# Attention beside a gated MLP on one core: gate weights on another queue, the first block split, and a new order of the attention stage

## The chip, the cores and the metric

The kernel runs on one core of one Trainium2 chip. The time is the device time of one execution in microseconds (us); the figure for a kernel is the median over its runs. The engines are named as the profile names them: PE is TensorE (PEld its weight loads), DVE is VectorE, ACT is ScalarE, POOL is GpSimd and SP is SyncE, which here only issues DMA transfers.

## What is computed

Both branches take the same normalised input `xn` (2048 tokens, 512 features, bf16); their outputs and the input itself are added.

```python
xn = layernorm(x)                                    # no weights
# branch A: 32 heads of 16, each query sees itself and the 255 keys before it
q, k, v = split(xn @ wqkv)
p = softmax(where(0 <= i - j < 256, q @ k.T * 16 ** -0.5, -1e9))
A = (p @ v) @ wo
# branch B: F = 1376, Fh = 688
z = gelu_tanh(xn @ w_in)
z1, z2 = z[:, :688], layernorm(z[:, 688:])
g = w_sp @ z2 + b_sp[:, None]                        # w_sp is 2048 x 2048
B = (z1 * g) @ w_out
out = x + A + B
```

## The kernel before

Tokens are cut into 16 blocks of 128. The program has two stages, and in both every engine's instructions run in the order in which they are written; nothing is rescheduled.

**The z stage** (the first 53 us). For each block `n` the input is loaded (`load_block` and `load_x`, SP's queue), its mean and variance are taken (`stats`, L257: two DVE instructions, then `rpow`, L117: one DVE instruction for variance plus epsilon and one POOL power for the reciprocal root), it is normalised (`norm`, L263, DVE, which waits for POOL), transposed to `xnT` (`transpose_x`, L274, four PE transposes into a PSUM tile and one ACT copy; from block 6 on a DMA transpose instead) and multiplied with the two halves of `w_in` (`do_z`, L284: four chunks of 128 features, each as two matmuls of 512 and 176 columns, then one ACT activation). Half 1 of z is normalised again (`z2_stats`, `z2_norm`, DVE and POOL). `w_in` comes in four transfers (`load_win`, L206): half 1 in chunks 0-1 and 2-3, which the first z needs, and half 0 in two more. One-element memsets into `w_in_sb` (L318) and `wqkv` (L332) hold later transfers back until DVE has come to them. The first nine projections of q, k and v run between the later blocks.

Ahead of it stands a warm-up: ten matmuls of 512 columns on a tile of zeros that DVE has set, then block 0's transposes, then three more.

The head of the z stage, as it is written:

```python
warm_up(N_WARM[0]); stats(0); ...
stats(1); norm(0); transpose_x(0); warm_up(N_WARM[1])
norm(1); transpose_x(1); do_z(0, 1)
stats(2); norm(2); stats(3); ...
do_z(1, 1); transpose_x(2); stats(4); norm(3); do_z(0, 0)
```

**The attention stage** (from 53 us on) runs the list of words in `ORDER` one by one. Only PE's work is ordered by it directly; the other engines take their parts in the same order.

- a number: so many steps of the mix `w_sp @ z2` (`mix`, L394; 512 steps of 344 columns, a DVE operation behind every sixteenth)
- `qTTe`: a group of scores, tile TT (four 128x128 blocks), one half of the heads (`scores`, L476): eight or more matmuls on 32 rows each, four at a time, into two PSUM tiles, and two exponentials on ACT. The pool of these tiles has three buffers
- `mTT`: the tile's masks, on POOL for diagonal blocks and on DVE for the far ones
- `a`, `A`, `B`, `C`: one group of values (`values`, L529), column-split matmuls, then on DVE and POOL the division (`divide`); the letter names the PSUM it goes to: `a` the one-buffer bank `ps_y`, the others a tile of the scores' pool
- `t`: the transpose of a finished value group (DVE)
- `p`, `P`: one projection, into `ps_y` or (`P`) a tile of the scores' pool
- `o`, `O`: half of an output block (four matmuls with `wo`, or six with `w_out`, a DVE addition and the store), in `ps_y` or in the scores' pool

Of the kernel before, what the change touches and what calls it, by code (L numbers as in the profile page):

```python
# [8 lines left out]
P = 128  # L9
BF = mybir.dt.bfloat16  # L10
F32 = mybir.dt.float32
# [8 lines left out]
FH = 688  # L20
FQ = FH // 2
NB = S_TOK // P
NDC = D // P
# [8 lines left out]
X_DMA = 6  # L32
LAST = 128
ONB = 4
N_WARM = (10, 3)

# [8 lines left out]


ORDER = """
pv11 Pk03 q000 1 pq03 2 q001 2 pq10 1 q010 9 m00 q011 1 pk10 q020 3 m01 2 a00 1 q021 10 q030  # L50
pk11 4 m02 q031 10 q040 2 pv03 q041 4 m03 t 1 pk12 q050 6 m04 1 q051 1 a01 3 q060 pk13 3 m05
q061 4 a02 1 q070 8 q071 a03 1 t 3 q080 pv10 2 m07 2 q081 pq11 3 m06 1 q090 pq12 4 q091 a04 3
m08 q100 2 pk20 2 q101 9 q110 pv12 1 t 1 m10 3 q111 1 pv13 1 m09 q120 5 pq21 q121 3 t 1 a05 m11
q130 2 m12 8 q131 pq20 4 q140 t t 2 pk21 q141 3 A06 a07 A10 q150 4 m13 7 q151 2 pq13 q160 m14 6
a11 q161 3 t 6 q170 1 t pv20 1 t q171 3 m16 5 m15 3 q180 4 pq23 q181 1 m17 8 q190 t a12 6 q191 1
pk23 3 m18 3 q200 6 m19 4 q201 a13 C14 B15 q210 t 2 pv21 4 q211 5 m20 3 q220 2 pk22 Pv23 3 m21
q221 3 pq31 q230 10 q231 pq30 2 m23 q240 4 pq22 2 m22 q241 7 t 1 q250 a16 1 t 3 q251 1 m24 2 t 3
Pv30 6 q260 pk32 3 t q261 2 A20 a17 A21 q270 11 q271 m26 pk30 4 q280 t 10 q281 2 pv31 4 q290 1
m25 2 m28 7 q291 2 pv22 q300 1 m27 9 q301 m29 6 A22 m30 a23 q310 8 q311 3 t 5 pk33 q320 1 m31
Pq33 3 a24 q321 2 t 7 t q330 3 pq32 t Pk31 q331 pv33 4 q340 2 m32 3 m33 3 q341 4 pv32 m34 1 q350  # L60
2 t 10 q351 3 a30 A25 t A26 a27 q360 10 q361 3 t o 1 q370 1 m35 1 o m36 q371 3 m37 5 t q380 3 o
1 q381 4 o q390 A31 a32 1 t 2 t 1 t q391 8 m39 q400 3 o 1 q401 o 1 O q410 2 O 1 o 3 m38 q411 1 o
q420 1 m40 5 A33 a34 q421 O t 2 O 1 q430 2 t m42 m41 o 1 q431 2 o q440 m43 4 O 2 O 1 A35 a36
q441 3 O m44 O o o t 5 A37 1 t O O t 2 o o 1 O O 6 O 1 O O O O O
"""


# [1 line left out]
def kernel(  # L69
# [12 lines left out]
    nc = tc.nc  # L82
# [6 lines left out]
    xnT = pers.tile([P, NDC, S_TOK], BF, name="xnT")  # L89
# [18 lines left out]
    ps_s = ctx.enter_context(tc.tile_pool(name="ps_s", bufs=3, space=bass.MemoryType.PSUM))  # L108
    ps_y = ctx.enter_context(tc.tile_pool(name="ps_y", bufs=1, space=bass.MemoryType.PSUM))
    ps_g = ctx.enter_context(tc.tile_pool(name="ps_g", bufs=1, space=bass.MemoryType.PSUM))  # L110
    sml = ctx.enter_context(tc.tile_pool(name="sml", bufs=3))
# [5 lines left out]
    def rpow(dst, var, n):  # L117
        v = sml.tile([P, NB], F32, name="rs_v")
        nc.vector.tensor_scalar(out=v[:, :n], in0=var, scalar1=LN_EPS, scalar2=None, op0=ALU.add)  # L119
        nc.gpsimd.tensor_tensor(out=dst, in0=v[:, :n], in1=negh[:, :n], op=ALU.pow)  # L120
# [57 lines left out]
    with tc.tile_pool(name="win_pool", bufs=1) as winp, tc.tile_pool(  # L178
        name="xsp", bufs=8
    ) as xsp, tc.tile_pool(name="xnp", bufs=4) as xnp:  # L180
        w_in_sb = winp.tile([P, NDC, F], BF, name="w_in_sb")
        zeros = winp.tile([P, 512], BF, name="zeros")
        nc.vector.memset(zeros[:], 0.0)  # L183
        nc.vector.memset(fmask[:], 1.0)
        nc.vector.memset(esel[:], 1.0)
        make_identity(nc, ident[:])
        xs_tiles = {}
# [3 lines left out]
        def load_block(n):  # L191
            if n % 2 == 0:
                xs_pairs[n // 2] = xsp.tile([P, 2, D], BF, name="xs")
            xs_tiles[n] = xs_pairs[n // 2][:, n % 2, :]
            nc.sync.dma_start(out=xs_tiles[n], in_=x2[n * P : (n + 1) * P, :])
# [7 lines left out]
            for j in range(2):  # L203
                xs_tiles[2 * n2 + j] = xs[:, j, :]

        def load_win(half, c0, c1):  # L206
            nc.sync.dma_start(
                out=w_in_sb[:, c0:c1, half * FH : (half + 1) * FH],
                in_=B_w_in[c0 * P : c1 * P, half * FH : (half + 1) * FH].rearrange(
                    "(c p) f -> p c f", p=P  # L210
                ),
            )

        load_block(0)
        load_block(1)
        load_win(1, 0, 2)
        load_block(2)
        load_win(1, 2, 4)
        load_block(3)
        warm = sml.tile([P, 1], F32, name="warm")  # L220
# [3 lines left out]
            out=fmask[:], in_=fmask[:], pattern=[[-1, P]], compare_op=ALU.is_gt,  # L224
# [3 lines left out]
            out=esel[:], in_=esel[:], pattern=[[-32, 4]], compare_op=ALU.is_ge,  # L228
# [3 lines left out]
            out=esel[:], in_=esel[:], pattern=[[32, 4]], compare_op=ALU.is_ge,  # L232
# [15 lines left out]
        def warm_up(n):  # L248
            wt = ps_s.tile([P, 2, 512], F32, name="warm_t", tag="S")
            for i in range(n):  # L250
                nc.tensor.matmul(  # L251
                    wt[:, 0, :], lhsT=zeros[:, 0:P], rhs=zeros[:], start=True, stop=True
                )

        xn_tiles = {}

        def stats(n):  # L257
            st = sml.tile([P, nc.vector.BN_STATS_DIM], F32, name="st")
            nc.vector.bn_stats(out=st[:], in_=xs_tiles[n])
            nc.vector.bn_aggr(out=mvx[:, n, :], in_=st[:])  # L260
            rpow(rstdx[:, n : n + 1], mvx[:, n, 1:2], 1)

        def norm(n):  # L263
            xn = xnp.tile([P, D], BF, name="xn")
            nc.vector.tensor_scalar(
                out=xn[:], in0=xs_tiles[n], scalar1=mvx[:, n, 0:1],
                scalar2=rstdx[:, n : n + 1], op0=ALU.subtract, op1=ALU.mult,
            )
            if n >= X_DMA:
                nc.sync.dma_start_transpose(out=xnT[:, :, n * P : (n + 1) * P], in_=xn[:])  # L270
            else:
                xn_tiles[n] = xn

        def transpose_x(n):  # L274
            xn = xn_tiles.pop(n)
            pool, tag = (ps_y, "y") if n == 1 else (ps_g, "g")
            tp = pool.tile([P, NDC, P], BF, name="tp", tag=tag)
            for c in range(NDC):
                nc.tensor.transpose(  # L279
                    out=tp[:, c, :], in_=xn[:, c * P : (c + 1) * P], identity=ident[:]  # L280
                )
            nc.scalar.copy(out=xnT[:, :, n * P : (n + 1) * P], in_=tp[:])

        def do_z(n, half):  # L284
            zp2 = ps_s.tile([P, 2, 512], F32, name="zs", tag="S")
            zp = zp2[:].rearrange("p a q -> p (a q)")
            f0 = half * FH
            for c in range(NDC):
                for lo, hi in Z_RANGES:
                    nc.tensor.matmul(  # L290
                        zp[:, lo:hi],
                        lhsT=xnT[:, c, n * P : (n + 1) * P],
                        rhs=w_in_sb[:, c, f0 + lo : f0 + hi],
                        start=(c == 0),
                        stop=(c == NDC - 1),
                    )
            dst = z1_all if half == 0 else z2_all
            nc.scalar.activation(out=dst[:, n, 0:FH], in_=zp[:, 0:FH], func=ACT.Gelu_apprx_tanh)  # L298

# [14 lines left out]
        early = [(kind, 0, grp) for grp in range(3) for kind in "kqv"]  # L314

        warm_up(N_WARM[0])
        stats(0)
        nc.vector.memset(w_in_sb[0:1, 0, 0:1], 0.0)  # L318
        load_x(2)
        load_win(0, 0, 2)  # L320
        load_win(0, 2, 4)
        stats(1)
        norm(0)
        transpose_x(0)
        warm_up(N_WARM[1])
        norm(1)
        transpose_x(1)
        do_z(0, 1)
        stats(2)
        norm(2)  # L330
        stats(3)
# [3 lines left out]
        for n2 in range(4, NB // 2):  # L335
            load_x(n2)
        do_z(1, 1)
        transpose_x(2)
        stats(4)
        norm(3)  # L340
        do_z(0, 0)
        nc.vector.tensor_reduce(
            out=emask[:, 0:1], in_=esel[:], op=ALU.add, axis=mybir.AxisListType.X
        )
        nc.vector.tensor_scalar(
            out=emask[:, 1:2], in0=emask[:, 0:1], scalar1=-1.0, scalar2=1.0,
# [232 lines left out]
    def finish():  # L579
# [9 lines left out]
        out=w_out_sb[:, 0:5, :], in_=B_w_out[0:640, :].rearrange("(c p) n -> p c n", p=P)  # L589
# [52 lines left out]
```

## Time and profile before

| | us |
|---|---|
| median of 3 runs | 265.3 (265.15 to 265.53) |
| the profiled execution | 265.24 |
| its span (first to last instruction) | 263.5 |
| PE busy in the span | 256.9 |
| ACT busy | 205.5 |
| DVE busy | 197.9 |
| POOL busy | 122.0 |
| first z matmul | 6.91 |
| first score group | 55.0 |

"Busy" for PE counts a matmul from its start to its modelled end, so it says that the engine had work in hand, not that it ran at its peak. The chain that ended last is followed back from the last instruction to whatever released it; an engine with nearly all of that chain sets the time. In the timeline a row gives start, duration, engine, line and operation, what is written from what is read, and in brackets the idle time in front of it with its releaser.

### The profile page before, as it was taken

What the parts mean: (1) busy time and instruction counts of PE and PEld (TensorE: products, weight loads), DVE (VectorE), ACT (ScalarE), POOL (GpSimd) and SP (SyncE); (2) the same over time, 40 slices, a digit from 0 to 9 for tenths busy, and PEclk for the clock granted to TensorE, in tenths of its full rate; (3) what the DMA queues carried; (4) which work ended last, traced back from release to release, by engine and by line L of the source; (5) the groups of instructions that cost most, each with busy time, mean ns of one, the idle gap of its engine ahead of it and who ended that gap; (6) DMA issues with size and microseconds to landing.
All of it is one profiled execution on the core that took longest, in us unless ns stands there. A gap on an engine that the chain in (4) does not pass through costs nothing.

```text
span 263.5 us, 7433 instructions
## 1 busy us (share of the span) xinstructions
PE 256.9 (98%) x3166; PEld 143.4 (54%) x3199; DVE 197.9 (75%) x384; ACT 205.5 (78%) x233; POOL 122.0 (46%) x140
## 2 busy tenths in 40 slices
PE   8999999999999999999999999999999999999995
PEld 3665665654546465555565456655564454545542
DVE  5899999667786888788797778897869563786542
ACT  2777767699999999999988989988898996782000
POOL 4334446116542573768553556455468453355100
PEclk9999999999999999999999999999999999999999
DMA  7892233940505073130360322661329263636432
GB/s 215 277 301 42 42 56 68 166 161 2 109 4 112 7 105 41 43 82 13 69 82 2 80 44 41 76 51 38 82 86 179 59 132 94 140 93 151 107 85 77
DMA packets 61233, 23.83 MB, mean 90 GB/s; under 512 B 52321, under 2 KB 60689, under 8 KB 61201
## 3 DMA queue, kind: packets, MB, share of 16 engines
q1 hardware_dynamic: 60720, 23.06, 41.1%
q8 instruction: 25, 0.41, 0.7%
q10 hardware_dynamic: 432, 0.30, 0.4%
q0 software_dynamic: 48, 0.00, 0.3%
q14 instruction: 8, 0.06, 0.1%
HBM read 8.41 MB, written 2.10 MB: 40 GB/s over the span
## 4 chain that ended last, share of the span: by engine, by line
PE 97%; issue 1%; DVE 1%; DVEq 0%
PE gf L402 31%; PE zs L290 14%; PE S L496 12%; PE m L151 10%; PE o_t L549 8%; PE fo L439 8%; PE m L135 6%; PE fo L433 5%; PE warm_t L251 2%; PE tp L279 1%; DVE xnT L444 0%; DVE o_c L565 0%; DVE zeros L183 0%; DVEq L565 0%
## 5 line engine op out<-in xcount | busy, mean ns | idle before, releaser
L504 ACT ACTIVATE E<-S 128x1024 bf16<-128x1024 f32 x180 | 168.9, 1042 | 16.9 <-PE S L496 9.1
L402 PE MATMUL gf<-z_all,wspT 128*128 128x344 bf16 x512 | 95.1, 311 | 0.1
L515 POOL TENSOR_SCALAR_AFFINE_SELECT E<-E 128x1024 bf16<-128x1024 bf16 x64 | 79.3, 1262 | 31.3 <-ACT E L504 31.1
L402 PEld LDWEIGHTS <-wspT 128*128 128x128 bf16 x512 | 44.1, 98 | 35.9 <-issue 15.4
L520 DVE TENSOR_TENSOR E<-E,fmask 128x1024 bf16<-128x1024 bf16 x56 | 53.0, 973 | 2.4 <-ACT E L504 2.3
L571 POOL TENSOR_TENSOR o_norm<-o_c,rsum 128x256 bf16<-128x256 f32 x32 | 21.5, 672 | 61.9 <-DVE rsum L569 59.2
L290 PE MATMUL zs<-w_in_sb,xnT 128*128 128x512 bf16 (+1 forms) x249 | 39.1, 307 | 0.4
L496 PE MATMUL S<-q_ring,k 32*128 32x128 bf16 (+2 forms) x760 | 37.2, 267 | 0.0
L298 ACT ACTIVATE z_all<-zs 128x688 bf16<-128x688 f32 x32 | 23.8, 744 | 12.5 <-PE zs L290 12.5
L151 PE MATMUL m<-xnT,wqkv 128*128 128x512 bf16 x111 | 31.5, 380 | 1.0 <-issue 0.2
L290 PEld LDWEIGHTS <-xnT 128*128 128x128 bf16 x256 | 22.2, 98 | 14.9
L409 DVE SCALAR_TENSOR_TENSOR z_all<-gf,b_all,z_all 128x344 bf16<-128x344 f32 x32 | 18.1, 567 | 14.6 <-PE gf L402 14.6
L565 DVE STREAM_TRANSPOSE o_c<-o_t 128x512 f32<-128x512 f32 x32 | 22.3, 698 | 7.2 <-PE o_t L549 6.5
L496 PEld LDWEIGHTS <-k 32*128 32x128 bf16 x760 | 12.7, 92 | 25.9 <-issue 25.2
L444 DVE TENSOR_TENSOR xnT<-fo,xnT 128x512 bf16<-128x512 f32 (+2 forms) x17 | 11.2, 659 | 17.0 <-PE fo L439 15.3
L549 PE MATMUL o_t<-E,v 128*32 128x128 bf16 (+1 forms) x1080 | 23.4, 238 | 0.0
L439 PE MATMUL fo<-w_out_sb,uT 128*128 128x512 bf16 (+2 forms) x101 | 23.3, 366 | 0.1
L549 PEld LDWEIGHTS <-v 128*32 128x32 bf16 x1080 | 19.2, 97 | 5.1 <-issue 4.6
L171 DVE TENSOR_TENSOR k<-m,emask 128x1024 bf16<-128x1024 f32 x13 | 15.8, 1218 | 3.1 <-PE m L151 3.0
L120 POOL TENSOR_TENSOR rstdx<-rs_v,negh 128x1 f32<-128x1 f32 x16 | 10.2, 640 | 17.0 <-DVE rs_v L119 14.5
L151 PEld LDWEIGHTS <-wqkv 128*128 128x128 bf16 x128 | 11.7, 98 | 11.6 <-issue 1.7
L135 PE MATMUL m<-wqkv,xnT 128*128 128x128 bf16 x256 | 16.9, 219 | 0.2 <-DVE o_c L565 0.2
(51 smaller groups left out, 174.6 us busy)
## 6 DMA issues: line engine op xcount, KB each, us to landing
xnT<-in_A_x_dram SPq DMA_DIRECT2D x4, 512.0 KB, 4.6
out_dram<-xnT SPq DMA_DIRECT2D x13, 128.0 KB, 1.8
xs<-in_A_x_dram SPq DMA_DIRECT2D x6, 256.0 KB, 6.8
wqkv<-in_A_wqkv_dram SPq DMA_DIRECT2D x1, 1536.0 KB, 6.4
w_in_sb<-in_B_w_in_dram SPq DMA_DIRECT2D x4, 344.0 KB, 4.2
w_out_sb<-in_B_w_out_dram SPq DMA_DIRECT2D x1, 640.0 KB, 6.1
xs<-in_A_x_dram SPq DMA_DIRECT2D x4, 128.0 KB, 2.7
wo_sb<-in_A_wo_dram SPq DMA_DIRECT2D x1, 512.0 KB, 4.9
```

What stands on the lines that cost most here:

```text
L135: nc.tensor.matmul(m[:, j * P : (j + 1) * P], lhsT=xnT[:, c, n * P : (n + 1) * P], rhs=wqkv[:, c, 2 * D + G * P : 2 * D + (G + 1) * P], st ...
L151: nc.tensor.matmul(m, lhsT=wqkv[:, c, w0 : w0 + P], rhs=xnT[:, c, grp * 512 : (grp + 1) * 512], start=(c == 0), stop=(c == NDC - 1),)
L290: nc.tensor.matmul(zp[:, lo:hi], lhsT=xnT[:, c, n * P : (n + 1) * P], rhs=w_in_sb[:, c, f0 + lo : f0 + hi], start=(c == 0), stop=(c == NDC ...
L298: nc.scalar.activation(out=dst[:, n, 0:FH], in_=zp[:, 0:FH], func=ACT.Gelu_apprx_tanh)
L402: nc.tensor.matmul(gf[:, 0:FQ], lhsT=wsp_tiles[n][:, c, :], rhs=z2_all[:, c, lo : lo + FQ], start=(c == 0), stop=(c == NB - 1),)
L439: nc.tensor.matmul(fo[:, c0:c1], lhsT=uT_tiles[n][:, c, :], rhs=w_out_sb[:, c, c0:c1], start=False, stop=(c == NFC - 1),)
L496: nc.tensor.matmul(S[:, h2, j * P : (j + w) * P], lhsT=k_t[(G, kb // 4)][32 * s : 32 * s + 32, e, (kb % 4) * P : (kb % 4 + 1) * P], rhs=q_ ...
L504: nc.scalar.activation(out=E[:, j : j + 3 : 2, 0:nb, :].rearrange("p h b c -> p h (b c)"), in_=tiles[pr][:, :, 0 : nb * P], func=ACT.Exp, ...
L515: nc.gpsimd.affine_select(out=E[:, :, j, :], in_=E[:, :, j, :], pattern=[[0, 8], [1, P]], compare_op=ALU.is_ge, fill=0.0, base=0, channel_ ...
L520: nc.vector.tensor_tensor(out=E[:, :, j, :], in0=E[:, :, j, :], in1=fmask[:].unsqueeze(1).to_broadcast([P, 8, P]), op=ALU.mult,)
L549: nc.tensor.matmul(T[32 * s : 32 * s + 32, e, j * P : (j + l) * P], lhsT=v_t[(G, kb // 4)][:, kb % 4, s, e : e + 2, :].rearrange("p a d -> ...
L565: nc.vector.transpose(out=C[:, 0 : 32 * DH], in_=Tb)
```

## The change

- The warm-up reads a constant of ones instead of a tile of zeros; the tile and its memset are gone, and the second warm-up has two matmuls instead of three.
- The first transfer of `w_in` (half 1, chunks 0-1) is issued on ACT's queue instead of SP's, behind a one-element DVE memset that is new.
- `stats` is split: `sums` is its first instruction and can be called ahead. Block 1's sums stay where its statistics were, and the rest of them comes behind block 0's transposes and copy. Likewise block 4's sums come ahead of `norm(3)` and the rest behind it.
- Block 0's copy to `xnT` is split: chunks 0-1 by ACT, chunks 2-3 by DVE.
- The first z (block 0, half 1) is split: chunks 0-1, then block 1's transposes, then chunks 2-3.
- `ORDER` is another list with the same score groups, masks, mix steps, projections, value groups and output parts. Value groups are `a` 18, `A` 6, `B` 4, `C` 4 instead of 19, 11, 1, 1; output parts are `o` 12, `O` 20 instead of 14 and 18; five projections go to the scores' pool in both.

```diff
-N_WARM = (10, 3)
+N_WARM = (10, 2)
 ORDER = """
-pv11 Pk03 q000 1 pq03 2 q001 2 pq10 1 q010 9 m00 q011 1 pk10 q020 3 m01 2 a00 1 q021 10 q030
...
-q420 1 m40 5 A33 a34 q421 O t 2 O 1 q430 2 t m42 m41 o 1 q431 2 o q440 m43 4 O 2 O 1 A35 a36
-q441 3 O m44 O o o t 5 A37 1 t O O t 2 o o 1 O O 6 O 1 O O O O O
+pk10 Pq03 q000 2 pv10 1 q001 3 pk03 q010 2 m00 8 q011 pq10 m01 3 q020 3 pk11 2 q021 8 q030 a00 7
...
+o q421 o 1 m41 q430 2 O 1 O o 3 q431 2 o 2 m42 1 m43 t q440 O 2 O A35 a36 q441 O O t 1 t O O O O
+o m44 o A37 1 O O O t O O O O O
 """
...
-        zeros = winp.tile([P, 512], BF, name="zeros")
-        nc.vector.memset(zeros[:], 0.0)
+        ones_w = nc.const_aps.tensor(1.0, [P, P], BF)
+        ones_m = nc.const_aps.tensor(1.0, [P, 512], BF)
...
-        def load_win(half, c0, c1):
-            nc.sync.dma_start(
+        def load_win(half, c0, c1, queue=nc.sync):
+            queue.dma_start(
...
         load_block(0)
         load_block(1)
-        load_win(1, 0, 2)
+        nc.vector.memset(w_in_sb[0:1, 0, FH : FH + 1], 0.0)
+        load_win(1, 0, 2, nc.scalar)
         load_block(2)
...
-                    wt[:, 0, :], lhsT=zeros[:, 0:P], rhs=zeros[:], start=True, stop=True
+                    wt[:, 0, :], lhsT=ones_w, rhs=ones_m, start=True, stop=True
...
+        st_tiles = {}
+
+        def sums(n):
+            st_tiles[n] = sml.tile([P, nc.vector.BN_STATS_DIM], F32, name="st")
+            nc.vector.bn_stats(out=st_tiles[n][:], in_=xs_tiles[n])
+
         def stats(n):
-            st = sml.tile([P, nc.vector.BN_STATS_DIM], F32, name="st")
-            nc.vector.bn_stats(out=st[:], in_=xs_tiles[n])
+            if n not in st_tiles:
+                sums(n)
+            st = st_tiles.pop(n)
...
-            nc.scalar.copy(out=xnT[:, :, n * P : (n + 1) * P], in_=tp[:])
+            dst = xnT[:, :, n * P : (n + 1) * P]
+            if n == 0:
+                nc.scalar.copy(out=dst[:, 0:2, :], in_=tp[:, 0:2, :])
+                nc.vector.tensor_copy(out=dst[:, 2:4, :], in_=tp[:, 2:4, :])
+            else:
+                nc.scalar.copy(out=dst, in_=tp[:])
...
-        def do_z(n, half):
-            zp2 = ps_s.tile([P, 2, 512], F32, name="zs", tag="S")
-            zp = zp2[:].rearrange("p a q -> p (a q)")
+        def do_z(n, half, c0=0, c1=NDC):
+            if c0 == 0:
+                zp_open[n] = ps_s.tile([P, 2, 512], F32, name="zs", tag="S")
+            zp = zp_open[n][:].rearrange("p a q -> p (a q)")
...
-            for c in range(NDC):
+            for c in range(c0, c1):
...
+            if c1 < NDC:
+                return
...
-        stats(1)
+        sums(1)
         norm(0)
         transpose_x(0)
         warm_up(N_WARM[1])
+        stats(1)
         norm(1)
+        do_z(0, 1, 0, 2)
         transpose_x(1)
-        do_z(0, 1)
+        do_z(0, 1, 2, NDC)
...
         transpose_x(2)
+        sums(4)
+        norm(3)
         stats(4)
-        norm(3)
         do_z(0, 0)
```

More of the change, by code (lines that the diff above doesn't have):

```diff
@@ L49 @@
 ORDER = """
-pv11 Pk03 q000 1 pq03 2 q001 2 pq10 1 q010 9 m00 q011 1 pk10 q020 3 m01 2 a00 1 q021 10 q030
[L51 to L61, printed above, removed]
@@ L62 @@
-1 q381 4 o q390 A31 a32 1 t 2 t 1 t q391 8 m39 q400 3 o 1 q401 o 1 O q410 2 O 1 o 3 m38 q411 1 o
-q420 1 m40 5 A33 a34 q421 O t 2 O 1 q430 2 t m42 m41 o 1 q431 2 o q440 m43 4 O 2 O 1 A35 a36
-q441 3 O m44 O o o t 5 A37 1 t O O t 2 o o 1 O O 6 O 1 O O O O O
+pk10 Pq03 q000 2 pv10 1 q001 3 pk03 q010 2 m00 8 q011 pq10 m01 3 q020 3 pk11 2 q021 8 q030 a00 7
+q031 2 m02 7 q040 pq11 4 q041 2 pv03 1 t 4 q050 5 a01 q051 4 m03 1 m04 3 q060 3 pv11 1 q061 4
+pk13 q070 9 m05 1 q071 pq13 3 q080 t 3 a02 q081 2 m07 7 m06 1 q090 a03 6 q091 pq12 2 q100 4 m08
@@ new lines @@
+pk12 1 q101 9 q110 m09 a04 5 q111 2 t 6 q120 1 m10 2 pk20 1 q121 4 t 1 A05 a06 q130 10 q131 m12
+pk21 m11 3 q140 6 t t 5 q141 2 pk22 q150 5 t 1 Pv20 m13 6 q151 A10 a07 1 Pq22 q160 3 m15 a11
+q161 4 m16 6 q170 6 pq20 q171 t 5 m14 5 q180 pv12 2 q181 4 a12 q190 1 m17 5 a13 q191 9 q200 1
+pv21 m18 2 q201 3 pk30 t 2 q210 1 m19 5 t 3 q211 pq23 C14 B15 q220 3 pq21 2 q221 2 m20 6 q230 3
+pv22 t q231 8 t 3 t 1 q240 1 m21 3 pq31 q241 1 m23 3 m22 pv13 3 q250 6 m24 3 q251 a20 C16 B17 3
+q260 2 pk23 t q261 t 11 m26 q270 pv30 2 t 4 q271 10 m27 Pv31 q280 pk31 m25 4 q281 t 12 q290 a21
@@ new lines @@
+A22 3 m28 2 q291 pv32 2 q300 t 4 pq33 q301 5 a23 m29 q310 8 q311 pq30 4 q320 3 t t 1 pq32 q321 2
+m30 4 pk32 q330 m31 10 q331 a24 A25 2 Pv23 q340 4 m33 3 m32 2 q341 pv33 5 q350 pk33 3 q351 1 m34
+2 t 8 t q360 2 a30 C26 B27 q361 5 t m35 6 q370 3 o 1 q371 1 o q380 2 m36 5 t 2 q381 3 a31 q390 4
+o q391 4 m37 2 t t o q400 m38 O 1 m39 O 4 q401 1 o 3 m40 1 o q410 C32 B33 t a34 q411 8 q420 t 8
+o q421 o 1 m41 q430 2 O 1 O o 3 q431 2 o 2 m42 1 m43 t q440 O 2 O A35 a36 q441 O O t 1 t O O O O
+o m44 o A37 1 O O O t O O O O O
@@ L281, in transpose_x @@
                 )
-            nc.scalar.copy(out=xnT[:, :, n * P : (n + 1) * P], in_=tp[:])
-        def do_z(n, half):
-            zp2 = ps_s.tile([P, 2, 512], F32, name="zs", tag="S")
-            zp = zp2[:].rearrange("p a q -> p (a q)")
+            dst = xnT[:, :, n * P : (n + 1) * P]
[4 more added lines that the diff above has]
+                nc.scalar.copy(out=dst, in_=tp[:])
+        zp_open = {}
+        def do_z(n, half, c0=0, c1=NDC):
+            if c0 == 0:
+                zp_open[n] = ps_s.tile([P, 2, 512], F32, name="zs", tag="S")
+            zp = zp_open[n][:].rearrange("p a q -> p (a q)")
             f0 = half * FH
-            for c in range(NDC):
+            for c in range(c0, c1):
                 for lo, hi in Z_RANGES:
```

## The prediction

> **What bounds the kernel now.** I read the page first, then the busy time by stretches, then the first 13 us in order of time, then the pieces of the chain. The page's busy totals and the shares of the chain that ended last:
>
> ```profile
> PE 256.9 (98%) x3166; PEld 143.4 (54%) x3199; DVE 197.9 (75%) x384; ACT 205.5 (78%) x233; POOL 122.0 (46%) x140
> ...
> PE 97%; issue 1%; DVE 1%; DVEq 0%
> ```
>
> TensorE (PE) is the bound from end to end, so only two things can move the time: the PE's own work, and moments in which it stands still. The stretches say where it does (columns: us of the stretch, then busy us of PE):
>
> ```profile
> 0.00:6.90 6.90, 5.64 (x21) 2.32 (x22) 3.74 (x13) 2.07 (x3) 3.11 (x13) 1.00 0.73 221
> 6.90:10.80 3.90, 3.90 (x33) 2.28 (x31) 3.02 (x12) 2.55 (x4) 1.43 (x3) 1.00 0.81 257
> 10.80:55.00 44.20, 43.83 (x329) 27.00 (x337) 39.42 (x120) 31.66 (x46) 17.25 (x29) 1.00 0.56 135
> 55.00:100.00 45.00, 44.49 (x563) 23.65 (x569) 34.11 (x49) 44.95 (x50) 21.29 (x20) 1.00 0.28 55
> 100.00:150.00 50.00, 49.63 (x765) 28.12 (x771) 40.53 (x65) 47.29 (x51) 27.49 (x27) 1.00 0.30 54
> 150.00:200.00 50.00, 49.68 (x793) 29.84 (x796) 40.81 (x67) 43.91 (x48) 28.19 (x28) 1.00 0.39 66
> 200.00:240.00 40.00, 39.63 (x533) 19.90 (x538) 26.83 (x45) 31.96 (x34) 19.34 (x19) 1.00 0.53 108
> ```
>
> Useful PE work starts at 6.69 us, and from 6.90 to 55 the PE is idle for 0.37 us. From 55 to 240, the attention stage but for its tail, it is idle 0.51 + 0.37 + 0.32 + 0.37 = 1.57 us. A head that is late by x us is therefore late at the end by x: nothing behind it has room. In the head itself, the rows that matter:
>
> ```profile
> 3.70 0.18 DVE L260 BATCH_NORM_AGGREGATE mvx<-st 128x2 f32<-128x6 f32 x1
> 4.00 0.69 DVE L259 BATCH_NORM_STATS2 st<-xs 128x6 f32<-128x512 bf16 x1
> 5.01 0.41 DVE L265 TENSOR_SCALAR xn<-xs,mvx,rstdx 128x512 bf16<-128x512 bf16 x1
> 5.17 0.66 POOL L120 TENSOR_TENSOR rstdx<-rs_v,negh 128x1 f32<-128x1 f32 x1 [0.45 <-DVE rs_v L119]
> 5.87 0.41 DVE L265 TENSOR_SCALAR xn<-xs,mvx,rstdx 128x512 bf16<-128x512 bf16 x1 [0.46 <-POOL rstdx L120]
> 6.17 0.59 ACT L282 COPY xnT<-tp 128x512 bf16<-128x512 bf16 x1 [3.87 <-PE tp L279]
> 6.69 0.39 PE L279 MATMUL tp<-ident,xn 128*128 128x128 bf16 x4
> 6.91 2.50 PE L290 MATMUL zs<-w_in_sb,xnT 128*128 128x512 bf16 x16
> 10.31 0.41 DVE L265 TENSOR_SCALAR xn<-xs,mvx,rstdx 128x512 bf16<-128x512 bf16 x1
> 10.77 0.40 PE L279 MATMUL tp<-ident,xn 128*128 128x128 bf16 x4
> ```
>
> Blocks 0 and 1 go through VectorE (DVE) side by side: block 1's aggregate, its power on GpSimd (POOL) and its norm (5.87) run while block 0 is transposed, so block 1's transpose (6.69) stands ready before the first z matmul (6.91). Block 3's norm, 10.31 to 10.72, is what the PE waits for at 10.77, and only by 0.13 us: DVE has no reserve there.
>
> **The change in the head.** *Warm-up.* The matrix of ones is a constant that POOL has written by 0.47 us, so the ten matmuls begin about 0.82 instead of 1.26 and end near 5.07 instead of 5.50 (pitch 0.43 between their weight loads). This frees the PE before block 0's norm is ready. The 13th warm-up lay under ACT's copy (6.17 to 6.76); leaving it out is worth nothing.
>
> *Gate weights on ACT's queue.* DVE's one-element memset now ends about 1.12 (fmask 0.17 and esel 0.06 from 0.93, then 0.06); SP's issue after such a memset came 0.1 us behind it, so ACT issues near 1.22 for some 0.43, and only then loads its table (1.28) and runs the dummy activation (0.20): 3.15 instead of 2.30. POOL's selects on esel and its memset wait for that and end about 4.14 instead of 3.29; the first power needs POOL at 4.16. Hidden, by 0.02 us; if the issue takes 0.2 longer, block 0 is late by that. SP's later issues move up by about 0.5 us. Nothing waited for these weights (the first z waited for block 1's transposes), so their early landing earns nothing. It may cost: block 0 lands just before its statistics at 2.98, and the weights' packets may now be among its own. Bounds 0 and +0.25 us; I take 0, since block 0 was issued 0.4 us sooner.
>
> The Trainium skill speaks against this part: "DMA: Bandwidth & Descriptors", section "Issuing engines are not separate DMA queues", says that transfers from several engines interleave on the same 16 DMA engines and that a second issuer saves issue time alone. By it the upper bound, +0.25 us, would hold; no run here shows it yet.
>
> *Block 0 ahead of block 1.* In the order of the built program DVE now runs: statistics of 0 and the raw sums of 1, norm of 0, then its half of block 0's copy, and only then aggregate, variance and (through POOL) norm of 1. And its half-copy waits for ACT's half-copy, not for the transposes. Step by step: norm 0 follows the power (4.16 + 0.56) at 4.77 instead of 5.01 and ends 5.18. Transposes from 5.26, four at a cold 0.11, ACT's copy 0.35 after the last start as before: 5.93. Its half costs about 0.36 (from 0.59 for 512 columns and 0.74 for the 688 of the z activation: 0.9 ns a column and 0.13 fixed): 6.29. z of block 0, first half, may start at 6.36, 0.55 earlier than before, and is over at 6.95 (four of sixteen matmuls that took 2.33). DVE's half, 6.34: no row shows it. Between 0.15 (DVE's smallest operations) and 0.69 (its 512-column cast out of PSUM); half that cast's columns give about 0.40, which I take: 6.74. Then block 1 as the rows of block 0 had it: aggregate 6.76, variance +0.22, power +0.24 (7.22) for 0.56, norm +0.05 (7.83) for 0.41: 8.24 instead of 6.28. Behind that norm stand the PE's transposes of 1 (8.30 instead of 6.69), behind them z's second half (8.53 to 9.11) and, through ACT's copy of 1 (8.72 to 9.31), z of block 1: 9.36 instead of 8.08. That is 1.28 us lost.
>
> DVE stays late: block 2's sums start at 8.22 instead of 6.20, and its norm, in the same steps, ends 10.39; sums of 3 to 11.06, aggregate 11.08, variance 11.30, sums of 4 (now ahead of norm 3) to 12.07, norm 3 from 12.14 to 12.55. The PE, done with z of block 0 at 11.93, waits for it and transposes block 3 at 12.60 instead of 10.77: **+1.83 us**. After it, norm 4 (about 14.5) and norm 5 (about 17.0) are ready before the PE asks (15.17, 17.73). The projection weights, gated on a DVE memset, go out 2.1 us later and land near 17.9; the first projection comes at about 21.4. So the loss stays at 1.83; the bounds of DVE's half-copy make it 1.58 to 2.12, a late block 0 up to 2.37.
>
> **The change in the attention stage.** Both orders hold the same tokens (512 mix steps, 90 score groups, 39 projections, 32 value groups, 32 output parts), so PE work differs only where it turns from full-array matmuls to the row-split scores or column-split values. Such a turn costs about 0.10 us: in the chain
>
> ```profile
> 64.32 1.56 PE gf L402 x10
> 67.20 0.58 PE gf L402 x4
> ```
>
> four mix steps behind full-array matmuls take 0.58 (0.146 each), ten behind a score group 1.56, 0.10 over ten times that. Counted through both orders there are 202 turns before and 200 after: **-0.2 us**. The rest can only come out of standing still, 1.57 us at most as read above. The one-buffer PSUM bank is what both orders crowd: adding row durations between its users, the next one comes with less than 0.5 us to spare behind DVE's copy of the last in 12 places before and 4 after. Value groups stand behind the last scores they need by at least 5.08 before and 4.95 after, and tile buffers come free with at least 0.10 before and 0.75 after. So waits become fewer rather than more. Bounds: all of it gone (-1.57), or as many new waits as one bad place of each kind (+0.5); I take -0.3, a fifth of it, because ACT stays as full as it is (44.95 of 45 us).
>
> **Sum**: 1.83 - 0.2 - 0.3 = +1.3 on the profiled run's own 265.24 (span 263.5 and 1.7 around it), which lies 0.1 under the median of 265.3: **266.6 us**.
>
> **Rivals.** (1) *The order pays for the head.* Place: the attention stage from 55 us on. If all 1.57 us of idle PE go with the turns, it nets +0.06: 265.3, no change. For it: fewer tight places. Against: the idle is spread over the stage in pieces of about 0.01 a us in both halves, with no one wait to remove. (2) *Faster: PE's busy time in the scores hides waits too.* The score group at 61.81 takes 0.60 in the chain where its neighbours take 0.34; from 2.4 us of idle, hidden waits and turns together the head is overpaid by what can be told; with 2.7 off it ends at 264.4. Few such groups are to be seen. (3) *The clock turns late.* Warm-up matmuls go at 0.43, z's at full rate. With fewer warm-ups and the PE idle from 6.95 to 8.30, the first z's could run cold: until about 9.6 us that hides behind norm 3; one more 3.4 us of it would make z of 1 and 0 last 2.3 us longer, some 2.2 past norm 3: 268.8. The Trainium skill, "TensorE: Matmul & The Clock Gate", Part 1, has the clock released by one busy window of about 3.4 us and withdrawn after an idle one; by it a gap of 1.3 us does nothing, and no run here shows the opposite. (4) *New waits in the order*, a score group held for its PSUM slot or a value for its mask, at 0.26 each as in (2): with no gain beside them, five to eight make 268.2 to 269.0.
>
> **How the numbers follow.** Forecast 0.66, rival 1 0.12, rival 2 0.07, rival 3 0.05, rival 4 0.10. A measurement here can tell 0.2%, 0.53 us, from none. Faster is rival 2: 0.07. Same is rival 1 and the forecast's low edge (0.03): 0.15. Slower is the rest: 0.78. Range 265.1 (rival 1, and 0.2 of rival 2's hidden waits) to 267.9 (head 2.37, turns -0.2, waits +0.5); the forecast's own is 266.0 (head 1.58, waits -0.6) to 267.4 (head 2.37, no waits saved).
>
> **What would show it.** Block 1's transposes about 8.3 us, the PE idle ahead of them for 1.3 us and ahead of block 3's by 0.7; DVE's half-copy starting behind ACT's; PE idle from 57 us on below 1.6 us. I am wrong if block 1's norm ends before 7 us, or if the attention stage shortens by more than 1.3 us.

## The result

Six runs of each kernel:

| | before | after |
|---|---|---|
| median, us | 265.5 (265.15 to 265.77) | 266.76 (266.26 to 267.46) |
| ratio | 1 | 1.0049, 95% interval 1.0033 to 1.0065 |
| the profiled execution, us | 265.24 | 266.77 |
| its span, us | 263.5 | 264.6 |
| block 3's transposes begin | 10.77 | 12.90 |
| last z matmul begins | 53.07 | 55.19 |
| last two additions begin (DVE, on the last output parts) | 259.71 | 261.14 |

The change makes the kernel slower by 0.5%. The last three rows cut the profiled difference of 1.53 us into its parts: the head is 2.13 us later, the stages of z and projections in between keep that (2.12), the attention stage gives 0.69 us back (206.64 us before, 205.95 after, from the last z matmul to the last two additions), and 0.10 comes in what lies behind.

The page of the kernel after, its busy totals and the shares of the chain that ended last by engine:

```profile
PE 256.3 (97%) x3167; PEld 142.5 (54%) x3198; DVE 197.9 (75%) x385; ACT 205.5 (78%) x233; POOL 125.3 (47%) x140
...
PE 76%; DVE 15%; issue 3%; POOL 2%; DMA 1%; SPq 0%; ACT 0%; POOLq 0%
```

The chain now runs over DVE for 15% where it had 1%. That is no new bound: it is followed back through the last releaser, and at a wait, however small, it jumps to the engine that ended it. The busy time by stretches, with the same columns as before, says what it cost. The last four rows are the attention stage: the first of them begins and the last one ends 1.83 us later than the rows of before, 1.83 being the loss that was forecast for the head:

```profile
0.00:6.90 6.90, 4.89 (x16) 1.65 (x16) 2.22 (x9) 1.77 (x3) 2.38 (x12) 1.00 0.72 231
6.90:10.80 3.90, 2.84 (x20) 1.44 (x20) 2.34 (x9) 1.42 (x3) 1.11 (x2) 1.00 0.66 222
10.80:55.00 44.20, 43.47 (x323) 26.65 (x328) 40.34 (x124) 31.31 (x46) 17.30 (x29) 1.00 0.52 116
56.83:100.00 43.17, 42.61 (x537) 22.64 (x541) 31.49 (x47) 42.59 (x47) 21.42 (x18) 1.00 0.28 63
100.00:150.00 50.00, 49.68 (x779) 28.57 (x783) 39.98 (x67) 46.75 (x51) 28.58 (x27) 1.00 0.29 54
150.00:200.00 50.00, 49.69 (x728) 29.25 (x731) 40.85 (x63) 45.36 (x49) 29.31 (x27) 1.00 0.24 54
200.00:241.83 41.83, 41.57 (x581) 21.42 (x588) 29.01 (x49) 33.03 (x35) 20.47 (x19) 1.00 0.56 112
```

From 6.90 to 10.80, where the PE had no idle moment before, it now stands still for 1.06 us, and from 10.80 to 55 for 0.73 instead of 0.37, half of that again in front of block 3. The four rows of the attention stage hold 0.56 + 0.32 + 0.31 + 0.26 = 1.45 us of idle, against 1.57.

The head of the kernel after, in order of time (start, us, engine, line and operation, output from input, and in brackets the idle time before it):

```profile
1.15 0.45 ACTq L207 DMA_DIRECT2D w_in_sb<-in_B_w_in_dram  x1
...
5.12 0.69 DVE L262 BATCH_NORM_STATS2 st<-xs 128x6 f32<-128x512 bf16 x1 [1.12 <-DMA xs<-in_A_x_dram]
...
5.73 0.40 DVE L273 TENSOR_SCALAR xn<-xs,mvx,rstdx 128x512 bf16<-128x512 bf16 x1
...
6.18 0.40 PE L287 MATMUL tp<-ident,xn 128*128 128x128 bf16 x4 [1.17 <-DVE xn L273]
6.62 0.37 ACT L292 COPY xnT<-tp 128x256 bf16<-128x256 bf16 x1 [3.49 <-PE tp L287]
7.02 0.29 DVE L293 COPY xnT<-tp 128x256 bf16<-128x256 bf16 x1 [0.90 <-ACT xnT L292]
...
8.27 0.41 DVE L273 TENSOR_SCALAR xn<-xs,mvx,rstdx 128x512 bf16<-128x512 bf16 x1 [0.68 <-POOL rstdx L120]
...
8.73 0.40 PE L287 MATMUL tp<-ident,xn 128*128 128x128 bf16 x4 [0.94 <-DVE xn L273]
...
12.43 0.41 DVE L273 TENSOR_SCALAR xn<-xs,mvx,rstdx 128x512 bf16<-128x512 bf16 x1
...
12.90 0.40 PE L287 MATMUL tp<-ident,xn 128*128 128x128 bf16 x4 [0.36 <-DVE xn L273]
```

The second row is the surprise. Block 1's raw sums, which ran at 4.00 before, wait for block 1's data (1.12 us) until 5.12. The chain of waits has that transfer as a piece of its own (start, us, what):

```profile
1.27 3.83 DMA xs<-in_A_x_dram
```

In DVE's queue these sums stand ahead of norm 0, so norm 0, whose power POOL has ready at 4.64, runs at 5.73 instead of the 4.77 that was worked out. The rest is the sequence of the prediction: DVE's half-copy behind ACT's, block 1's norm at 8.27 instead of 5.87, its transposes at 8.73 with the PE idle before them, block 3's norm at 12.43, and the PE waiting for it until 12.90.

### The profile page after: what moved, and what is told of

The parts are those of the page before. It is cut to its first block, busy times and chain, and to the rows that moved or that the text cites. A ratio compares the mean times of both kernels' runs of the same rounds, so it can differ in the third digit from the quotient of the medians.

```text
span 264.6 us, 7426 instructions
## 1 busy us (share of the span) xinstructions
PE 256.3 (97%) x3167; PEld 142.5 (54%) x3198; DVE 197.9 (75%) x385; ACT 205.5 (78%) x233; POOL 125.3 (47%) x140
## 4 chain that ended last, share of the span: by engine, by line
PE 76%; DVE 15%; issue 3%; POOL 2%; DMA 1%; SPq 0%; ACT 0%; POOLq 0%
PE gf L423 31%; PE S L517 11%; PE o_t L570 8%; PE m L151 8%; PE fo L460 8%; PE fo L454 5%; PE m L135 5%; DVE st L321 4%; DVE st L262 3%; DVE xn L273 2%; DVE z_all L327 2%; DMA xs<-in_A_x_dram 1%; DVE mv L322 1%; DVE mvx L268 1%; DVE rs_v L119 1%
## 5 line engine op out<-in xcount | busy, mean ns | idle before, releaser
L423 PE MATMUL gf<-z_all,wspT 128*128 128x344 bf16 x512 | 92.7, 310 | 0.1
L536 POOL TENSOR_SCALAR_AFFINE_SELECT E<-E 128x1024 bf16<-128x1024 bf16 x64 | 82.4, 1313 | 21.7 <-ACT E L525 21.6
L592 POOL TENSOR_TENSOR o_norm<-o_c,rsum 128x256 bf16<-128x256 f32 x32 | 22.2, 693 | 73.0 <-DVE rsum L590 71.2
L316 ACT ACTIVATE z_all<-zs 128x688 bf16<-128x688 f32 x32 | 23.8, 744 | 12.4 <-PE zs L306 12.4
L517 PEld LDWEIGHTS <-k 32*128 32x128 bf16 x760 | 12.4, 92 | 25.6 <-issue 24.0
```

The source lines that it names most:

```text
L423: nc.tensor.matmul(gf[:, 0:FQ], lhsT=wsp_tiles[n][:, c, :], rhs=z2_all[:, c, lo : lo + FQ], start=(c == 0), stop=(c == NB - 1),)
L517: nc.tensor.matmul(S[:, h2, j * P : (j + w) * P], lhsT=k_t[(G, kb // 4)][32 * s : 32 * s + 32, e, (kb % 4) * P : (kb % 4 + 1) * P], rhs=q_ ...
L536: nc.gpsimd.affine_select(out=E[:, :, j, :], in_=E[:, :, j, :], pattern=[[0, 8], [1, P]], compare_op=ALU.is_ge, fill=0.0, base=0, channel_ ...
```

## The experiments

Unless a ratio says otherwise, it is to the kernel before, run beside it on the same chip (medians of before: 265.25 to 265.28 us), with its 95% interval. "Block 3" is the start of its transposes; "stage" is the time from the last z matmul to the last two additions. With the start of before, block 3 varies from 10.63 in e1 to 10.89 in e5, so differences under 0.2 us in it say nothing. What varies there is when block 0 lands: counted from block 0's statistics it is 7.79 us in before, 7.80 in e1 and 7.81 in e5. All of these kernels compute the whole of the reference.

### 1 and 2: the start and the order apart

```diff
 (e1: the kernel before, with the order of the kernel after)
 ORDER = """
-pv11 Pk03 q000 1 pq03 2 q001 2 pq10 1 q010 9 m00 q011 1 pk10 q020 3 m01 2 a00 1 q021 10 q030
...
+pk10 Pq03 q000 2 pv10 1 q001 3 pk03 q010 2 m00 8 q011 pq10 m01 3 q020 3 pk11 2 q021 8 q030 a00 7
...
```

e2 is the other half: the kernel after with the order of before.

> The head of the kernel before, with the new order of the attention stage. Theory A (the head lost 2.1 us, the new order wins 0.7 by itself): 0.7 us under the kernel before, about 264.7; block 3's transposes at 10.8 us, the attention stage (first projection to the last addition's start) 205.9 us as in the changed kernel, against 206.6 before. Rival (the stage is shorter only because it starts 2.1 us later, with its transfers further ahead): no difference to the kernel before, 265.4, and a stage of 206.6.

> The changed head with the old order of the attention stage. Theory A: block 3's transposes at 12.9 us and 2.1 us over the kernel before, about 267.5, with a stage of 206.6. Rival (a late start shortens any order): 1.4 over, about 266.8, with a stage of 205.9.

| | median, us | ratio | block 3 | stage |
|---|---|---|---|---|
| e1, old start, new order | 264.61 (264.33 to 264.78) | 0.9973 [0.9961, 0.9984] | 10.63 | 205.96 |
| e2, new start, old order | 267.24 (267.14 to 267.51) | 1.0076 [1.0061, 1.0092] | 12.73 | 206.64 |

The attention stage in one stretch, in the order before, after, e1, e2 (columns as above):

```profile
53.07:259.71 206.64, 204.97 (x2804) 112.70 (x2829) 151.99 (x242) 170.89 (x182) 100.94 (x97) 1.00 0.39 76
```
```profile
55.19:261.14 205.95, 204.39 (x2806) 112.35 (x2829) 152.00 (x242) 171.01 (x182) 104.53 (x97) 1.00 0.36 77
```
```profile
52.93:258.89 205.96, 204.40 (x2806) 112.34 (x2829) 151.97 (x243) 171.00 (x182) 104.48 (x97) 1.00 0.36 76
```
```profile
55.03:261.67 206.64, 204.97 (x2804) 112.71 (x2829) 151.97 (x242) 170.90 (x182) 100.84 (x97) 1.00 0.37 76
```

The length of the stage goes with the order alone, to 0.01 us, whether the head is early or late: a late start does not shorten it, and the order does not use the later start for anything. The two parts add up: 264.61 is 0.64 below its run of before and 267.24 is 1.99 above, which makes +1.35, against +1.26 for the whole change. Of the 0.69 us, only 0.11 was to be seen as idle PE (1.67 to 1.56); 0.58 left the PE's *busy* time, although both orders hold the same work.

### 3 and 4: the two changes of the head apart

```diff
 (e3: the kernel after, first gate weights back on SP's queue)
-        nc.vector.memset(w_in_sb[0:1, 0, FH : FH + 1], 0.0)
-        load_win(1, 0, 2, nc.scalar)
+        load_win(1, 0, 2)
```

```diff
 (e4: the kernel after, blocks 0 and 1 side by side again)
-            if n == 0:
-                nc.scalar.copy(out=dst[:, 0:2, :], in_=tp[:, 0:2, :])
-                nc.vector.tensor_copy(out=dst[:, 2:4, :], in_=tp[:, 2:4, :])
-            else:
-                nc.scalar.copy(out=dst, in_=tp[:])
+            nc.scalar.copy(out=dst, in_=tp[:])
...
-        sums(1)
+        stats(1)
         norm(0)
         transpose_x(0)
         warm_up(N_WARM[1])
-        stats(1)
         norm(1)
-        do_z(0, 1, 0, 2)
         transpose_x(1)
-        do_z(0, 1, 2, NDC)
+        do_z(0, 1)
...
-        sums(4)
-        norm(3)
         stats(4)
+        norm(3)
```

> The changed kernel with the first gate weights back on SP's queue, between blocks 1 and 2 as before, and without the memset that held them. Block 1 should land near 3.5 us and its sums start at 4.0. Theory A (both parts cost: block 1's late landing and DVE's new sequence): block 0's norm at 4.8, block 1's at 7.8, block 3's transposes near 12.4; 0.5 under the changed kernel, about 266.2. Rival B (the late landing is the whole loss): block 3's transposes near 10.8 and 2.1 under, 264.7.

> The changed kernel with the old sequence of blocks 0 and 1 (both statistics ahead of both norms, ACT's undivided copy, undivided first z, block 4's statistics in one piece); the weights stay on ACT's queue. Block 1 lands near 5.1. Theory A: both norms about 1.0 later than before (6.1 and 6.9), block 3's transposes near 11.8; 1.1 under the changed kernel, about 265.7. Rival C (DVE's new sequence is the whole loss): block 3's transposes near 10.8, 264.7. Rival B (the late landing is the whole loss): 12.9 and 266.8.

| | median, us | ratio | block 3 | stage |
|---|---|---|---|---|
| e3, DVE's new sequence alone | 265.74 (265.55 to 265.82) | 1.0013 [1.0004, 1.0022] | 12.03 | 205.96 |
| e4, weights on ACT's queue alone | 266.75 (265.79 to 267.24) | 1.0048 [1.0032, 1.0064] | 13.13 | 205.95 |

In e3's timeline (its lines are one lower than those of after) block 1's data is in time again:

```profile
4.08 0.69 DVE L261 BATCH_NORM_STATS2 st<-xs 128x6 f32<-128x512 bf16 x1
4.83 0.41 DVE L272 TENSOR_SCALAR xn<-xs,mvx,rstdx 128x512 bf16<-128x512 bf16 x1
...
12.03 0.40 PE L286 MATMUL tp<-ident,xn 128*128 128x128 bf16 x4 [0.36 <-DVE xn L272]
```

Norm 0 is at 4.83, 0.90 earlier than after, and block 3's transposes are 0.87 earlier. So the weights on ACT's queue delay the kernel through block 1's landing, and the new sequence by itself costs 12.03 - 10.77 = 1.26 us of the head, not 1.83. Block 3 lies between the two expectations of 12.4 and 10.8, so neither part is the whole loss.

e4's median is the one that rival B gave (the late landing is the whole loss, 266.8), but e3 has refuted that, and A and C stay below it. Its six executions lie in two heaps: 265.79 and 265.87, and 266.74 to 267.24. The stretches of the profiled one (266.95 us) and its first z matmuls:

```profile
5.00:7.60 2.60, 1.01 (x10) 0.53 (x10) 2.00 (x6) 0.58 (x1) 0.66 (x1) 1.00 1.08 371
7.60:11.00 3.40, 3.40 (x16) 1.75 (x14) 2.60 (x9) 1.33 (x2) 1.02 (x2) 0.50 0.53 184
11.00:14.00 3.00, 2.95 (x26) 2.00 (x26) 2.83 (x12) 1.97 (x4) 1.40 (x3) 1.00 0.80 201
```
```profile
7.67 4.15 PE L302 MATMUL zs<-w_in_sb,xnT 128*128 128x512 bf16 x16
```

The granted clock is 1.00, then 0.50 for 3.4 us, then 1.00 again: the clock that had been granted was taken back, after a stretch in which the PE worked for 1.01 of 2.60 us. Block 3's norm is over at 11.78 here, but the PE still works through cold z matmuls. So e4 measures the clock as well as the weights. The mean granted clock tells the executions in which that happened: 0.994 in this one and 0.992 in the one of 267.24 us. The two of 266.74 and 266.77 have 1.000, so nothing was taken back in them; what made them late has no trace.

### 6: the same with more warm-ups

```diff
 (e6: e4, and)
-N_WARM = (10, 2)
+N_WARM = (16, 4)
```

> The run with the old sequence of blocks 0 and 1 and the weights on ACT's queue, with 16 and 4 warm-up matmuls instead of 10 and 2, which lie in the time in which the PE waits for block 0's norm. Theory (the granted clock fell to half for 3.4 us because the PE was idle before block 0, in some executions of that run): the clock stays up, block 3's transposes stand at 11.8 us, all runs lie within 0.4 us of 265.7. Rival (the half clock has nothing to do with the warm-up): runs of 265.8 and of 266.7 to 267.2 as before.

265.74 us, 11 runs from 265.43 to 265.99 in one heap; ratio 1.0015 [1.0007, 1.0024]; block 3 at 11.73, stage 205.95. The sixteen first z matmuls:

```profile
7.76 2.50 PE L302 MATMUL zs<-w_in_sb,xnT 128*128 128x512 bf16 x16
```

2.50 us instead of 4.15 for the same work: in the profiled execution of e4 it was the clock. Without it, the weights on ACT's queue cost 11.73 - 10.77 = 0.96 us of the head: norm 0 stands behind the late statistics of block 1 and runs at 5.97 instead of 5.01. The two parts alone, 0.96 + 1.26 = 2.22, make nearly what both do together (2.13).

### 7 and 9: DVE's queue order

```diff
 (e7: the kernel after, block 1's remaining statistics ahead of the half-copy)
         norm(0)
+        stats(1)
         transpose_x(0)
         warm_up(N_WARM[1])
-        stats(1)
         norm(1)
```

```diff
 (e9: the kernel after, block 1's sums behind norm 0)
-        sums(1)
         norm(0)
+        sums(1)
         transpose_x(0)
```

> The changed kernel with block 1's aggregate, variance and power ahead of block 0's transposes, so that DVE's half of block 0's copy no longer stands before them; all else stays, the late block 1 too. Theory: block 1's norm starts at 7.35 instead of 8.27 us and its transposes come 0.9 sooner; block 3's transposes near 12.0 and 0.9 under the changed kernel, 265.9. Rival (block 1's late landing sets everything behind it): nothing changes, 266.8.

> The changed kernel with block 1's sums behind block 0's norm instead of ahead of it, so that the norm does not stand behind an instruction that waits for block 1's transfer. Theory: block 0's norm goes from 5.73 to about 4.75 us, block 1's from 8.27 to about 7.5, block 3's transposes to about 12.2; 0.7 under the changed kernel, 266.0. Rival (only block 1's chain matters, and it starts with its landing at 5.1 in any case): block 1's norm stays at 8.2 and the time at 266.8.

| | median, us | ratio | norm 0 | norm 1 | block 3 |
|---|---|---|---|---|---|
| after | 266.76 | 1.0049 | 5.73 | 8.27 | 12.90 |
| e7 | 265.81 (265.55 to 266.52) | 1.0023 [1.0011, 1.0036] | 5.79 | 7.50 | 12.61 |
| e9 | 265.88 (265.71 to 266.04) | 1.0020 [1.0011, 1.0029] | 4.80 | 7.57 | 12.20 |

In e9 the weights are issued as after, but norm 0 no longer stands behind a wait for block 1's data and runs at 4.80, as in e3:

```profile
4.80 0.41 DVE L273 TENSOR_SCALAR xn<-xs,mvx,rstdx 128x512 bf16<-128x512 bf16 x1 [0.68 <-POOL rstdx L120]
...
5.13 0.68 DVE L262 BATCH_NORM_STATS2 st<-xs 128x6 f32<-128x512 bf16 x1
...
5.26 0.61 PE L287 MATMUL tp<-ident,xn 128*128 128x128 bf16 x4
...
5.91 0.37 ACT L292 COPY xnT<-tp 128x256 bf16<-128x256 bf16 x1 [2.77 <-PE tp L287]
6.32 0.29 DVE L293 COPY xnT<-tp 128x256 bf16<-128x256 bf16 x1 [0.51 <-ACT xnT L292]
```

That gives back 0.70 of the 0.87 us which e3 gave back with the transfer itself: most of what the weights' move costs is not the late data but what is queued behind the wait for it. The rest is not the late data either, since the sums are over at 5.81 and the half-copy waits for ACT's half until 6.32. In e9's trace the clock turned full only at 6.56 us, and ACT's half-copy starts 0.65 us after the first transpose, where it is 0.44 in e3.

In e7 block 1's norm comes 0.77 us earlier, so the half-copy and its wait for ACT do hold block 1 back. But e7's runs split (265.55 to 265.81, and 266.37 to 266.52); in the profiled one, of 266.44, the clock was full only from 9.71 us, its first four z matmuls took 1.35 us instead of 0.76, and the PE came to block 3's transposes at 12.61 although that norm was over at 12.06. What e7's sequence is worth at a full clock has no trace.

### 8: is it ACT's queue, or the moment?

```diff
 (e8: the kernel after, and 0.5 us of DVE work ahead of the memset that holds the weights)
         load_block(1)
+        hold = winp.tile([P, 1024], BF, name="hold")
+        nc.vector.memset(hold[:], 0.0)
         nc.vector.memset(w_in_sb[0:1, 0, FH : FH + 1], 0.0)
         load_win(1, 0, 2, nc.scalar)
```

> The changed kernel with a memset of 0.53 us on DVE (a tile that nothing reads) ahead of the one that lets ACT issue the gate weights: they go out on ACT's queue at about 1.7 us, when SP issued them before, and no longer at 1.15. Theory (two queues share the engines, so the weights' packets stand among block 1's wherever they are issued from ACT): block 1 lands at 4.5 us or later, the time stays within 0.4 of 266.8. Rival (only the earlier issue did it): block 1 lands near 3.5, its sums start at 4.0, block 3's transposes near 12.0 as in the run with the weights on SP, 265.8.

266.23 us (266.21 to 266.42); ratio 1.0033 [1.0021, 1.0045]; block 3 at 12.58; stage 205.96. Its timeline (lines two to three higher than those of after):

```profile
1.65 0.47 ACTq L207 DMA_DIRECT2D w_in_sb<-in_B_w_in_dram  x1
2.15 1.28 ACT L224 ACT_TABLE_LOAD   x1 [2.15 <-DVE w_in_sb L218]
...
3.87 0.69 DVE L264 BATCH_NORM_STATS2 st<-xs 128x6 f32<-128x512 bf16 x1
...
4.60 0.56 POOL L120 TENSOR_TENSOR rstdx<-rs_v,negh 128x1 f32<-128x1 f32 x1
...
5.20 0.41 DVE L275 TENSOR_SCALAR xn<-xs,mvx,rstdx 128x512 bf16<-128x512 bf16 x1 [0.64 <-POOL rstdx L120]
```

Issued from ACT's queue 0.5 us later, the weights leave block 1 alone: its sums run at 3.87. That ACT's queue disturbs SP's whenever it is used falls; issuing the weights at 1.15, 0.12 us ahead of block 1's own issue on SP, is what delays block 1. But now the other side of the bargain shows: ACT's issue pushes its table load, the load its dummy activation, that POOL's selects, and these the first power, from 4.08 to 4.60. It is the step of which the prediction said that it was hidden by 0.02 us. Norm 0 is at 5.20, and of the 0.87 us that e3 gave back, 0.55 stay lost (12.58 against 12.03). Norm 0 explains 0.37 of them (5.20 against 4.83). The rest is the clock again, full only from 6.12 us here: ACT's half-copy starts 0.63 us after the first transpose, against 0.44 in e3.

### 5 and 10: a version that beats both

The new order's one wait that the profile shows, of after:

```profile
56.92 1.22 DVE L171 TENSOR_TENSOR k<-m,emask 128x1024 bf16<-128x1024 f32 x1
...
57.43 0.47 PE L423 MATMUL gf<-z_all,wspT 128*128 128x344 bf16 x2
58.06 0.68 DVE L161 CAST q_ring<-m 128x512 bf16<-128x512 f32 x1
58.19 1.05 PE L135 MATMUL m<-wqkv,xnT 128*128 128x128 bf16 x16 [0.29 <-DVE k L171]
```

The projection `pv10` needs the one-buffer PSUM bank and waits for DVE's copy of `pk10` out of it, 1.22 us long; it starts 0.76 us behind two mix steps. The projection beside it, `Pq03`, lies in the scores' pool and is copied in 0.68. e5 lets the two change places, on top of e1; e10 then puts `norm(3)` ahead of `stats(4)`, so that norm 3 does not stand behind block 4's sums and statistics.

```diff
 (e5: e1, and)
-pk10 Pq03 q000 2 pv10 1 q001 3 pk03 q010 2 m00 8 q011 pq10 m01 3 q020 3 pk11 2 q021 8 q030 a00 7
+pq03 Pk10 q000 2 pv10 1 q001 3 pk03 q010 2 m00 8 q011 pq10 m01 3 q020 3 pk11 2 q021 8 q030 a00 7
```

```diff
 (e10: e5, and)
-        stats(4)
         norm(3)
+        stats(4)
```

> The head of the kernel before with the new order, and in that order the first two projections change places and PSUM (pq03 in the one-buffer bank, Pk10 in the scores' pool), so that the bank is freed by a copy of 0.69 us and not by one of 1.22. Theory: the 0.46 us in which the PE stands before the first projection of v is gone and the stage lasts 205.5 us; 0.4 under the run of the old head with the new order, about 264.2. Rival (DVE is as late as before, and the next user of the bank waits instead): the wait shows up a few us later and the time stays at 264.6.

> The best run so far (old head, new order with the two projections swapped), and in the head block 3's norm ahead of block 4's statistics instead of behind them. Theory (the PE waits for block 3's norm by 0.1 us): block 3's transposes come with the end of the z before them, 0.1 sooner; 263.95. Rival (the z before it, or its weights' landing, ends just as late): 264.06, no difference.

e5: 264.06 us (263.92 to 264.15), ratio 0.9949 [0.9935, 0.9962], stage 205.50. e10: 263.95 us (263.78 to 264.09), ratio 0.9949 [0.9936, 0.9963], stage 205.50. In e5 the same projection follows the two mix steps without a wait:

```profile
55.41 0.47 PE L402 MATMUL gf<-z_all,wspT 128*128 128x344 bf16 x2
...
55.72 1.06 PE L135 MATMUL m<-wqkv,xnT 128*128 128x128 bf16 x16
```

It starts 0.31 us behind them instead of 0.76, which is 0.45, and the stage is shorter by 0.46. e10's trace has block 3's norm 0.41 us earlier (10.00) and its transposes at 10.47 instead of 10.89; their weight load (PEld) still waits for that norm:

```profile
10.00 0.41 DVE L265 TENSOR_SCALAR xn<-xs,mvx,rstdx 128x512 bf16<-128x512 bf16 x1 [0.66 <-POOL rstdx L120]
...
10.47 0.23 PEld L279 LDWEIGHTS <-xn 128*128 128x128 bf16 x4 [0.21 <-DVE xn L265]
```

Part of the 0.41 is no work of the edit (block 2's norm, ahead of it, is 0.13 earlier too, 7.92 against 8.05). Counted from block 0's statistics, the last z matmul begins after 49.89 us in e10 and after 50.09 to 50.10 in before, e1 and e5, so the one trace shows a gain of 0.2 us in the head. But the times of e10 and e5 overlap, and the executions neither show nor refute a gain of 0.1. Either is 0.5% faster than before and, by the ratios to it, about 1% faster than after.

## Why the prediction came out as it did

The forecast of 266.6 us and the signs of both parts were right. The sum was +1.33 and the profile shows +1.53: +0.30 in the head, -0.19 in the attention stage, +0.10 in the tail. The 0.30 of the head, however, hides two larger errors of opposite sign; that they nearly cancel is luck.

- *What bounds the kernel.* Right. The 2.13 us that block 3 lost were 2.12 us at the last z matmul, and in e1 to e10 the start of the stage and its length never influenced each other.
- *Warm-up.* Right in its times (0.85 and 5.02 after, 0.82 and 5.07 forecast). The clock turned full at 4.63 us after and at 4.81 in e3, against 6.15 before, but that is not the change's work: with the old warm-up it turned at 4.91 in e1, 4.24 in e5 and 4.51 in e10, with the new one at 6.12 in e8 and 6.56 in e9.
- *Gate weights on ACT's queue: "Bounds 0 and +0.25 us; I take 0".* This is the term that failed. Alone it costs 0.96 us (e6). The working looked at block 0's landing, which was in time (statistics at 2.90), and took block 1's for unchanged, though the paragraph on block 0 ahead of block 1 puts block 1's sums before norm 0. Of the Trainium skill, the section "Issuing engines are not separate DMA queues" in "DMA: Bandwidth & Descriptors" says that a second issuer saves issue time and nothing else; this case's traces agree, and go further. Issued at 1.15 us from ACT, the weights land at 4.98 to 5.36 (six traces); issued at 1.73 from SP, at 5.03 to 5.64 (five), so the earlier issue hardly brings them earlier. Block 1's 128 KB land at 4.77 to 5.15 in the six (after: 5.09) and at 3.32 to 3.58 in the five (before: 3.46).
- *Block 0 ahead of block 1: +1.83.* The mechanism was right step by step, its size too large: alone it costs 1.26 (e3). With the clock full from 4.81 on, ACT's half-copy starts 0.44 us after the first transpose instead of 0.67, so DVE's starts at 6.14 instead of 6.34 (this part goes with the execution: 0.65 in e9, whose clock turned late); it takes 0.29 us, not the 0.40 taken between 0.15 and 0.69; and block 1's norm is at 7.39 instead of 7.83. From there to norm 3 it is 4.16 us, where 4.31 were reckoned. That DVE waits for ACT's half and not for the transposes stands in the brackets: 0.90, from ACT.
- *Together* the two give 12.90 for block 3 where 12.60 was forecast: 0.57 too much for the sequence, and 0.87 not reckoned for the weights. Of the signs, block 1's transposes came at 8.73 with 0.94 us of idle PE ahead of them (8.3 and 1.3 were named), and 0.36 ahead of block 3's (0.7).
- *The attention stage: -0.2 for turns, -0.3 for waits.* Measured -0.69. Turns and waits were not taken apart by a run. The visible idle fell by 0.11 alone, so if the turns are worth their 0.2, some 0.4 was waiting that is counted as busy. One such place is in the trace of before, a score group of 0.66 us where most of its kind take 0.41:

```profile
60.29 0.41 PE L496 MATMUL S<-q_ring,k 32*128 32x256 bf16 x8
...
61.74 0.66 PE L496 MATMUL S<-q_ring,k 32*128 32x128 bf16 x8
```

Of the 82 groups of eight it is the only one over 0.5 before, and after there is none. That is what rival 2 named, at a size far below the 2.4 us that it needed. The new order has one wait of its own that the profile shows, worth 0.45 us (e5).

- *Rivals.* The order pays for a third of the head, not for all of it (1). One new wait came, not five to eight (4). The late or withdrawn clock (3) did not come in the profiled run, but one of the six executions, of 267.46 us, had a mean granted clock of 0.992, and e4 and e7 show what it is. The cost was worked out as 2.2 us past norm 3; the two executions of e4 with such a clock lie 1.1 to 1.5 us over its two fastest. The argument against it, that a gap of 1.3 us does nothing, was wrong in a head with few warm-ups: in e4 the PE's longest idle piece ahead of the cold stretch was 1.74 us, and in the 3.41 us ahead of it (4.20 to 7.61) the PE was busy for 1.63. The Trainium skill, "TensorE: Matmul & The Clock Gate", Part 1, has the half clock return after an idle window of about 3.4 us; the cold stretch of e4 is as long as that window, but the PE was not idle for one ahead of it, and there the measurement decides.

What stays open: why the weights' early issue delays block 1 by 1.6 us, rather than by the share of the bandwidth that their packets take. The runs show when it happens (issued at 1.15 us) and when not (1.65 from ACT, or behind block 1 on SP), not by what order the packets are served. The weights issued from SP ahead of block 1 were not run, so the queue and the order of issue are not taken apart for that case.

## What to carry to other kernels

When work is moved ahead in an in-order queue, ask of each instruction that stays in front of it when *its* data lands: here 0.9 of the 2.1 us lost in the head was a finished statistic standing behind a wait for another block, and in the rest block 1's statistics stood behind a copy that waited for ACT. Look at a transfer's neighbours before issuing it from a second queue: here it landed hardly earlier, and the one that lost was the one that the path needed. And where the bounding engine looks 98% busy, its busy time may still hold waits; measure a new order by the length of its stage, apart from everything else that the change brings.

## What was not expected of the hardware

- A granted PE clock was taken back for 3.4 us (0.50 from 7.6 to 11.0 in e4) with no idle piece over 1.74 us before it. In the 3.41 us between the grant (4.20) and the loss the PE was busy for 1.63. As long a stretch behind the grant held 1.97 us of work in the profiled run of after, 2.12 in e2, 2.24 in e3 and 2.35 in e8, and there the clock stayed.
- By the mean granted clocks this befell two of e4's six executions, one of the six of after and none of the 11 of e6, which has 16 + 4 warm-up matmuls instead of 10 + 2.
- In e7 the clock first turned full at 9.71 us, in the others whose trace was read between 4.1 and 6.6, with either head.
- Weights issued 0.58 us earlier landed hardly earlier (4.98 to 5.36 us against 5.03 to 5.64), and put back a small transfer beside them by more than 1 us (4.77 to 5.15 against 3.32 to 3.58).
